# Reordering two chains of block products: phase 2's first two products ahead of phase 1's last two, phase 2 pair by pair, and its operands' preparation in place and queued

## Chip, core and metric

The kernel runs on one core of one Trainium2 chip. Its time is device microseconds (us) of that core, the median of several executions. Time before the change: 851.96 us, median of 3 runs (849.39, 851.96, 854.7). The profile is of one execution of 852.34 us whose span, first to last instruction, is 850.6 us.

## The reference

The reference is a linear attention followed by a two-layer network with a gated activation, over 8 batches of 576 tokens, 8 heads of width 64:

```python
q_s = softmax(q, axis=-1)            # with + 1e-9 in the divisor
k_s = softmax(k, axis=2)             # over the tokens
kv  = einsum('bhsd,bhse->bhde', k_s, v)
x   = einsum('bhsd,bhde->bhse', q_s, kv)   # -> 4608 tokens x 512
h   = x @ w_in                        # 512 x 2048
g   = h * clip(h + 3, 0, 6) / 6
out = g @ w_out                       # 2048 x 512
```

The result is float32. The kernel multiplies each float32 operand as a high and a low part, so one product of blocks takes three matmul passes (high x high, and the two mixed ones).

## The kernel before, in words

**Two halves.** The first 1536 tokens (three blocks of 512) are multiplied plainly by the functions `gemm1` and `gemm2`, while weights are decoded and sums of weight blocks are made and written to DRAM. The other 3072 tokens are three *superblocks* s = 0, 1, 2 of 1024 tokens, and the loop `for s in range(NS)` at the end of the kernel (L796 to L814) runs `phase1(s, between1)` and then `phase2(s, between2)` for each.

**Products.** In a superblock each of the two matrix products is done over 2x2 blocks with seven block products instead of eight, on sums and differences of blocks. The 2048 middle columns are eight pairs p = 0..7, so each phase has 8 x 7 = 56 *slots* (p, n), n being the kind of product. A slot is six TensorE matmuls of 128x512: two column halves c times three passes m. The order of phase 1's slots is SLOTS1 (L393 to L395); it ends with (6,6), (7,4), (7,5), (7,6). Product (7,5) adds onto the PSUM bank in which (7,4) left its sum, after VectorE has read that sum at L554. The order of phase 2's slots is SLOTS2 (L396, L397): all eight pairs of kind 1, then of kind 2, 3, 0, 4, 6, 5. TensorE keeps the program's order from the second block on (`keep_in_program_order`, L79 to L93).

**Phase 1** multiplies weights (fetched from DRAM two slots at a time, six such groups ahead, `fetch` L457) by *factors*: seven tiles `right0` to `right6` made of the superblock's x by `factors(s)` (L482). Its results go from PSUM into the tiles g of pair p (`ga`, `gb`, four quarters a, b, c, d): copies by ScalarE (L545, L550, L552), additions by VectorE (L547, L554, L558), the gated activation `relu6` (L513 ScalarE, L514 VectorE) and a difference (L561).

**Phase 2** multiplies weights by *parts of g*. `make()` (L571) takes the next slot of SLOTS2, splits one quarter of g into high (ScalarE cast, L120) and low (VectorE subtraction, L121) into a ring of four buffers `gf`, and for kinds 1, 2 and 0 does one more VectorE operation on g in place (L582, L584, L586). `make()` is called three times ahead and then once per slot. Sums gather in PSUM: kinds 1, 3, 4 and 5 one after the other in the same two banks `xb`, kind 2 in two banks `yb`, kinds 0 and 6 in two banks `zb`. After pair 7 of a kind, the banks are read: ScalarE scales them into SBUF (L631, L637), VectorE adds two such tiles (L640) or scales and adds (`blend`, L602), and a DMA on SyncE's queue sends results out (`send`, L597). The SBUF tiles for that come from a pool named `v` with three buffers.

**Factors of the next superblock.** `factors(s+1)` is a generator of seven steps. In the order before: split X11; split X21; take a tile from the pool `v`, subtract into it (L497) and split it (T3); subtract twice in place (L500, L501) and split (T2); split (T1); split X22; subtract (L508) and split (T4). A split of such a tile is a ScalarE cast and a VectorE subtraction of 128x1024. A step is called after phase 2's slots 18, 21, 33, 36, 39, 42 and 45 (L808). The steps of the next superblock's attention (`sb_attention(s+1)`, 12 tiles of 128x1024 in all over the three) are called after the odd slots of phase 1 and the first odd ones of phase 2.

**Who sets the order.** TensorE's order is the program's. The order of VectorE's, ScalarE's and GpSimdE's instructions is laid down beforehand by a planner (`schedule_with_timeline_sim=True`, L872) that puts an instruction early where, by its own estimates, the engine is free and the operands are there; what stands in `tc.high_priority()` (the readings of PSUM) goes first. In the trace, three splits of factors (`right<-x`, L121) that the program calls after phase 2's slots 18, 21 and 42 run at 435.34, 437.64 and 447.89 us, the first two ahead of phase 2's first product.

Of the kernel before, what the change touches and what calls it, by code (L numbers as in the profile page):

```python
# [10 lines left out]
F32 = mybir.dt.float32  # L11
# [7 lines left out]
P = 128  # L19
# [13 lines left out]
def attention_moe(  # L33
# [39 lines left out]
    def bank(name):  # L73
        return ps.tile([P, TB], F32, name=name, tag="p")
# [42 lines left out]
    whole = dr.tile([P, NFC, 2 * DM], F32, name="whole")  # L117

    def split(hi, lo, src):
        nc.scalar.copy(hi, src)  # L120
        nc.vector.tensor_sub(lo, src, hi.bitcast(F32))  # L121

    def load_w(f):
        raws[f] = place(f, U32, f"raw_{f}")
# [268 lines left out]
    AT = {1: 0, 0: 1, 3: 3, 2: 4, 4: 6, 5: 9, 6: 12}  # L393
    SLOTS1 = sorted((7 * p + AT[n], p, n) for p in range(NPAIR) for n in range(7))
    SLOTS1 = [(p, n) for _, p, n in SLOTS1]  # L395
    ORDER2 = (1, 2, 3, 0, 4, 6, 5)  # L396
    SLOTS2 = [(p, n) for n in ORDER2 for p in range(NPAIR)]  # L397
    SLOT = [{pn: i for i, pn in enumerate(slots)} for slots in (SLOTS1, SLOTS2)]
    NSLOT = len(SLOTS1)

# [16 lines left out]
    def sum_weights(pair, side):  # L417
# [30 lines left out]
    ring = []  # L448

    come = {}  # L450
    wanted = iter(
        [(s, side, g) for s in range(NS) for side in range(2) for g in range(NSLOT // GROUP)]
    )

    turn = iter(range(10**6))
# [26 lines left out]
    def factors(s):  # L482

        x = x_of(s)
        x11, x12, x21, x22 = (x[:, 2 * a : 2 * a + 2, b * TH : (b + 1) * TH] for a in (0, 1) for b in (0, 1))

        def parts(n, src):
            t = place(n, F32R, f"right{n}").rearrange("p (e i n) -> p e i n", e=2, i=2)
            split(t[:, 0], t[:, 1], src)
            x_parts[s, n] = t  # L490

        parts(X11, x11)
        yield
        parts(X21, x21)
        yield
        t = moe.tile([P, 2 * DM], F32, name="v", bufs=3).rearrange("p (i n) -> p i n", i=2)
        nc.vector.tensor_sub(t, x22, x12)  # L497
        parts(T3, t)
        yield
        nc.vector.tensor_sub(x12, x12, x11)  # L500
        nc.vector.tensor_sub(x11, x22, x12)  # L501
        parts(T2, x11)
        yield
        parts(T1, x12)
        yield
        parts(X22, x22)
        yield
        nc.vector.tensor_sub(x21, x21, x11)  # L508
        parts(T4, x21)
        yield  # L510
# [2 lines left out]
        nc.scalar.activation(r, h, AF.Relu, bias=three, scale=1.0)  # L513
        nc.vector.scalar_tensor_tensor(g, r, 6.0, h, op0=ALU.min, op1=ALU.mult)  # L514

    def phase1(s, between):
        xb, yb, zb = {}, {}, {}
        for i, (p, n) in enumerate(SLOTS1):
            if n == 1:
                xb[p] = bank("x1")[:, 0:TH]  # L520
            if n == 2:
                yb[p] = bank("y1")[:, 0:TH]
            if n == 0:
                zb[p] = bank("z1")[:, 0:TH]
            to = zb[p] if n == 0 else yb[p] if n in (2, 6) else xb[p]
            w_hi, w_lo = (left(s, 0, i)[:, e] for e in (0, 1))
            f_hi, f_lo = (x_parts[s, ORDER[n][1]][:, e] for e in (0, 1))
            for c in range(2):
                cs = slice(c * P, (c + 1) * P)
                for m, (w_, f_) in enumerate(((w_hi, f_hi), (w_hi, f_lo), (w_lo, f_hi))):  # L530
                    mm(to, w_[:, cs], f_[:, c], n in (0, 1, 2) and not c and not m, c == 1 and m == 2, True)
            used(s, 0, i)
            if (s, p) not in g_pairs:
                t = place(7 + p, F32, f"g{p}")
                g_pairs[s, p] = t.rearrange("p (e n) -> p e n", e=2)
            ga, gb = (g_pairs[s, p][:, e] for e in (0, 1))
            h11, h12, h21, h22 = ga[:, 0:TH], ga[:, TH:], gb[:, 0:TH], gb[:, TH:]
            x, y, z = xb.get(p), yb.get(p), zb.get(p)

            def temp():  # L540
                return moe.tile([P, TB], F32, name="g", bufs=2)

            with tc.high_priority():
                if n == 1:
                    nc.scalar.copy(h11, x)  # L545
                if n == 0:
                    nc.vector.tensor_add(h11, h11, z)  # L547
                    relu6(h11, temp(), h11)
                if n == 3:
                    nc.scalar.copy(h21, x)  # L550
                if n == 2:
                    nc.scalar.copy(h22, y)  # L552
                if n == 4:
                    nc.vector.tensor_add(h22, h22, x)  # L554
                if n == 5:
                    relu6(h12, temp(), x)
                if n == 6:
                    nc.vector.tensor_add(h21, h21, y)  # L558
                    r = moe.tile([P, 2 * DM], F32, name="v", bufs=3)
                    relu6(gb, r, gb)  # L560
                    nc.vector.tensor_sub(h12, h22, h12)  # L561
            between(i)

    def phase2(s, between):
        if "g" not in held:
            held["g"] = xp.tile([P, 4, 2, TH], F32R, name="gf", tag="xa")
        ring = held["g"]
# [3 lines left out]
        def make():  # L571
            i, (p, n) = next(made, (None, (None, None)))
            if i is None:
                return
            ga, gb = (g_pairs[s, p][:, e] for e in (0, 1))
            a, b, c, d = ga[:, 0:TH], ga[:, TH:], gb[:, 0:TH], gb[:, TH:]
            src = {1: a, 2: b, 3: a, 0: c, 4: b, 6: c, 5: d}[n]
            t = ring[:, i % 4]
            split(t[:, 0], t[:, 1], src)
            ready[i] = t  # L580
            if n == 1:
                nc.vector.tensor_add(a, a, b)  # L582
            if n == 2:
                nc.vector.tensor_sub(b, d, a)  # L584
            if n == 0:
                nc.vector.tensor_sub(c, c, a)  # L586

        for _ in range(3):
            make()
        xb = [bank("x2")[:, 0:TH] for _ in range(2)]  # L590
        yb = zb = None
        sixth = 1.0 / 6.0
# [12 lines left out]
        for i, (p, n) in enumerate(SLOTS2):  # L605
            if p == 0 and n == 2:
                yb = [bank("y2")[:, 0:TH] for _ in range(2)]
            if p == 0 and n in (0, 6):
                zb = [bank("z2")[:, 0:TH] for _ in range(2)]
            to = zb if n in (0, 6) else yb if n == 2 else xb  # L610
            make()
            f_hi, f_lo = (ready[i][:, e] for e in (0, 1))
            w_hi, w_lo = (left(s, 1, i)[:, e] for e in (0, 1))
            for m, (w_, f_) in enumerate(((w_hi, f_hi), (w_lo, f_hi), (w_hi, f_lo))):
                for c in range(2):
                    mm(
                        to[c],
                        w_[:, c * P : (c + 1) * P],
                        f_,
                        p == 0 and m == 0 and n in (0, 1, 2, 6),  # L620
                        p == NPAIR - 1 and m == 2,
                        True,
                    )
            del ready[i]
            used(s, 1, i)
            if p == NPAIR - 1:
                with tc.high_priority():
                    if n in (1, 3, 5):
                        t = kept_out[n] = outs("o")
                        for c in range(2):  # L630
                            nc.scalar.mul(t[:, c], xb[c], sixth)  # L631
                        if n == 5:
                            send(t, 0, 1)
                    if n == 2:
                        t = kept_out[4] = outs("o")
                        for c in range(2):
                            nc.scalar.mul(t[:, c], yb[c], sixth)  # L637
                    if n == 3:
                        for c in range(2):
                            nc.vector.tensor_add(kept_out[3][:, c], kept_out[3][:, c], kept_out[4][:, c])  # L640
                    if n == 0:
                        for c in range(2):
                            blend(kept_out[1], zb, c)
                        send(kept_out[1], 0, 0)
                    if n == 4:
                        for c in range(2):
                            blend(kept_out[4], xb, c)
                        send(kept_out[4], 1, 1)
                    if n == 6:
                        for c in range(2):  # L650
                            blend(kept_out[3], zb, c)
                        send(kept_out[3], 1, 0)
            between(i)

# [139 lines left out]
    for s in range(NS):  # L796
        more = s + 1 < NS
        step = steps(sb_attention(s + 1), 6) if more else iter(())
        fac = factors(s + 1) if more else iter(())

        def between1(i):
            if i % 2:
                next(step, None)

        def between2(i):
            if i % 2 and i < 16:
                next(step, None)
            if i in (18, 21, 33, 36, 39, 42, 45):  # L808
                next(fac, None)

        phase1(s, between1)
        phase2(s, between2)
        for _ in fac:
            pass  # L814

# [62 lines left out]
```

## Time and profile before

| | |
|---|---|
| time, median of 3 | 851.96 us |
| the profiled execution, span | 852.34 us, 850.6 us |
| TensorE busy | 807.8 us (95%) |
| VectorE busy | 677.9 us (80%) |
| ScalarE busy | 442.6 us (52%) |
| phase 1, s = 0: first product | 347.67 us |
| phase 2: first product, s = 0, 1, 2 | 445.62, 614.22, 769.38 us |
| last matmul's start (phase 2 of s = 2) | about 845.5 us |

How to read it: PE is TensorE's matmuls, PEld its weight loads, DVE VectorE, ACT ScalarE, POOL GpSimdE, SP SyncE with the DMA queue. A line of a group or of the timeline names the source line, the engine, the operation, and written and read tiles by the program's names (x, y and z are the PSUM banks; `right` a factor, `gf` a part of g; `gp` and `left` are the buffers of fetched weights). `x6` is a count of instructions; what stands in brackets is the engine's idle time ahead of that line and what ended it. Matmuls overlap in the records: one is shown with some 390 ns, but the next starts about 0.227 us after it. A row of the chain that ended last gives start, length and what ran.

### The profile page before, as it was taken

How to read it: one execution, taken by the hardware profiler on the slowest of the kernel's cores; microseconds unless marked ns; L12 is line 12 of the kernel's file. 1: busy time of each engine (PE TensorE's matmuls, PEld its weight loads, DVE VectorE, ACT ScalarE, POOL GpSimd, SP SyncE). 2: the span in 40 equal slices, each digit the busy share in tenths (PEclk: the TensorE clock that was granted, in tenths of full speed). 3: DMA queues.
4: the chain of work that ended last, by engine and by line, in shares of the span. 5: the costliest groups of instructions: out<-in, count | busy, mean ns of one | idle time of the engine just before them, and what ended most of it. 6: DMA issues, size and time to landing. Idle time of an engine off the chain costs nothing.

```text
span 850.6 us, 11778 instructions
## 1 busy us (share of the span) xinstructions
PE 807.8 (95%) x4032; PEld 646.5 (76%) x4032; DVE 677.9 (80%) x1095; ACT 442.6 (52%) x717; POOL 66.1 (8%) x179
## 2 busy tenths in 40 slices
PE   4899989999999998999989999999999999999997
PEld 3677767777887786787768868777788788887886
DVE  7998998998878887589889984698688936658763
ACT  7997664443444553444546553545554535445542
POOL 5000011111101110001112000010000000000000
PEclk9999999999999999999999999999999999999999
DMA  9998686578469641788756667664556676665672
GB/s 367 413 401 298 236 272 207 192 263 274 149 201 344 221 165 52 226 279 288 267 177 198 193 215 237 220 227 158 166 189 194 229 241 195 198 195 176 199 234 87
DMA packets 75643, 192.30 MB, mean 226 GB/s; under 512 B 7232, under 2 KB 19520, under 8 KB 73536
## 3 DMA queue, kind: packets, MB, share of 16 engines
q1 hardware_dynamic: 75008, 190.51, 65.7%
q10 hardware_dynamic: 576, 1.05, 0.3%
q8 instruction: 32, 0.52, 0.3%
q14 instruction: 27, 0.22, 0.1%
HBM read 147.49 MB, written 44.04 MB: 225 GB/s over the span
## 4 chain that ended last, share of the span: by engine, by line
PE 63%; DVE 21%; DMA 5%; ACT 4%; issue 4%; POOL 2%; SPq 0%; ACTq 0%; DVEq 0%; POOLq 0%
PE x L87 26%; PE y L87 10%; PE z L87 9%; PE po L87 8%; PE ph L87 8%; DVE gp L121 2%; DVE g L514 2%; DMA qt<-in_qf_dram 2%; PE px L87 2%; POOL swap L303 2%; DVE v L141 1%; DMA kt<-in_kT_dram 1%; DVE v L145 1%; ACT qt L219 1%; PE pkv L87 1%
## 5 line engine op out<-in xcount | busy, mean ns | idle before, releaser
L120 ACT CAST gf<-g 128x512 fp32r<-128x512 f32 x168 | 104.1, 623 | 96.4 <-DVE gf L121 48.5
L87 PE MATMUL po<-w,gp 128*128 128x512 f32 x576 | 146.7, 401 | 5.5 <-ACT gp L120 2.8
L87 PE MATMUL ph<-x,w 128*128 128x512 f32 x576 | 143.8, 397 | 2.9 <-ACT w L120 2.6
L121 DVE TENSOR_TENSOR gf<-g,gf 128x512 fp32r<-128x512 f32 x168 | 112.9, 686 | 31.9 <-ACT gf L120 31.1
L87 PEld LDWEIGHTS po<-w,gp 128*128 128x128 f32 x576 | 106.0, 189 | 33.9 <-ACT gp L120 5.9
L87 PEld LDWEIGHTS ph<-x,w 128*128 128x128 f32 x576 | 108.6, 190 | 28.4 <-ACT w L120 3.3
L87 PE MATMUL x<-right,gp 128*128 128x512 f32 x384 | 96.3, 396 | 3.7 <-DVE g L554 3.7
L87 PE MATMUL x<-gf,gp 128*128 128x512 f32 x384 | 89.0, 389 | 0.0
L87 PEld LDWEIGHTS x<-right,gp 128*128 128x128 f32 x384 | 72.4, 190 | 20.2 <-DVE g L554 4.5
L87 PEld LDWEIGHTS x<-gf,gp 128*128 128x128 f32 x384 | 72.1, 188 | 15.0
L513 ACT ACTIVATE g<-ph,three 128x512 f32<-128x512 f32 x48 | 32.7, 686 | 67.0 <-PE ph L87 66.7
L513 ACT ACTIVATE v<-g,three 128x1024 f32<-128x1024 f32 x24 | 27.6, 1152 | 42.8 <-DVE g L558 42.8
L87 PE MATMUL x<-right,left 128*128 128x512 f32 x192 | 48.0, 393 | 1.7 <-DVE g L554 1.7
L87 PE MATMUL y<-right,gp 128*128 128x512 f32 x192 | 48.4, 397 | 0.0
L87 PE MATMUL z<-gf,gp 128*128 128x512 f32 x192 | 45.7, 392 | 0.9 <-DVE gf L121 0.7
L87 PE MATMUL x<-gf,left 128*128 128x512 f32 x192 | 44.8, 389 | 0.0
L120 ACT CAST gp<-g 128x512 fp32r<-128x512 f32 x48 | 29.7, 620 | 28.0 <-DVE g L514 27.8
L87 PEld LDWEIGHTS z<-gf,gp 128*128 128x128 f32 x192 | 35.7, 188 | 9.9 <-DVE gf L121 2.6
L87 PEld LDWEIGHTS x<-right,left 128*128 128x128 f32 x192 | 35.6, 188 | 10.0 <-DVE g L554 2.5
L87 PEld LDWEIGHTS y<-right,gp 128*128 128x128 f32 x192 | 35.9, 190 | 8.2 <-issue 0.5
L87 PEld LDWEIGHTS x<-gf,left 128*128 128x128 f32 x192 | 36.0, 188 | 7.5
L513 ACT ACTIVATE g<-g,three 128x512 f32<-128x512 f32 x24 | 17.4, 724 | 39.2 <-DVE g L547 39.2
(136 smaller groups left out, 1297.5 us busy)
## 6 DMA issues: line engine op xcount, KB each, us to landing
gp<-wf SPq DMA_DIRECT2D x112, 512.0 KB, 3.5
left<-wf SPq DMA_DIRECT2D x56, 512.0 KB, 3.5
raw<-in_w_dram SPq DMA_DIRECT2D x16, 1024.0 KB, 13.7
wf<-gp SPq DMA_DIRECT2D x64, 256.0 KB, 3.0
wf<-w SPq DMA_DIRECT2D x48, 256.0 KB, 4.1
vt<-in_v_dram SPq DMA_DIRECT2D x28, 325.0 KB, 5.7
kt<-in_kT_dram SPq DMA_DIRECT2D x28, 288.0 KB, 3.4
ke<-in_k_dram SPq DMA_DIRECT2D x24, 320.0 KB, 5.2
```

What stands on the lines that cost most here:

```text
L87: nc.tensor.matmul(out, lhsT, rhs, start=start, stop=stop, skip_group_check=goes_on)
L120: nc.scalar.copy(hi, src)
L121: nc.vector.tensor_sub(lo, src, hi.bitcast(F32))
L141: nc.vector.scalar_tensor_tensor(vu, high, 0xC0000000, m, op0=ALU.bitwise_and, op1=ALU.bitwise_or)
L145: nc.vector.tensor_tensor(vu, vu, low, op=ALU.add)
L219: nc.scalar.activation(qs[:, i], qs[:, i], AF.Exp, bias=qm[:, i : i + 1], accum_out=qr[:, i : i + 1],)
L303: nc.gpsimd.tensor_copy(swap[r : r + QD], stat[o : o + QD])
L513: nc.scalar.activation(r, h, AF.Relu, bias=three, scale=1.0)
L514: nc.vector.scalar_tensor_tensor(g, r, 6.0, h, op0=ALU.min, op1=ALU.mult)
```

## The change

Five edits, all in the superblocks:

1. **Order of the phases.** The functions `phase1` and `phase2` become generators that stop after each slot, and one list PHASES runs both: phase 1's slots 0 to 53, then phase 2's slots 0 and 1, then phase 1's slots 54 and 55 ((7,5) and (7,6)), then phase 2's from 2 on. The order in which weights are fetched follows that list. The first three `make()` are called ahead of phase 1's slot 50.
2. **Order of phase 2.** All pairs of kind 1; then pair by pair kinds 2 and 3 in turn; then pair by pair kinds 0 and 4; then kind 6; then kind 5.
3. **Factors without a temporary.** T1 = x12 - x11 and T2 = x22 - T1 are made in place, in the tile of x11, and T3 = x22 - x12 in that of x12; the order of steps is X11, X21, T1, T2, T3, X22, T4. There are as many operations as before (four subtractions, seven splits).
4. **Where factor steps are called.** After phase 2's slots 9, 13, 17, 23, 29, 35 and 41.
5. **Queued.** Each such step is traced inside `tc.issue_after` of the cast and the subtraction that the latest `make()` returned (`front`): none of the step's instructions may be planned ahead of them on ScalarE or VectorE. The factors of superblock 0, made during the plain blocks, have edit 3 but not this one.

```diff
     def split(hi, lo, src):
-        nc.scalar.copy(hi, src)
-        nc.vector.tensor_sub(lo, src, hi.bitcast(F32))
+        return nc.scalar.copy(hi, src), nc.vector.tensor_sub(lo, src, hi.bitcast(F32))
+
+    front = []
+
+    def behind(units, count=1):
+
+        with ExitStack() as order:
+            for ins in front:
+                order.enter_context(tc.issue_after(ins.ins))
+            for _ in range(count):
+                next(units, None)
...
-    ORDER2 = (1, 2, 3, 0, 4, 6, 5)
-    SLOTS2 = [(p, n) for n in ORDER2 for p in range(NPAIR)]
+    ORDER2 = ((1,), (2, 3), (0, 4), (6,), (5,))
+    SLOTS2 = [(p, n) for some in ORDER2 for p in range(NPAIR) for n in some]
...
+    PHASES = [(0, i) for i in range(NSLOT)] + [(1, i) for i in range(NSLOT)]
+    PHASES[NSLOT - 2 : NSLOT + 2] = PHASES[NSLOT : NSLOT + 2] + PHASES[NSLOT - 2 : NSLOT]
     wanted = iter(
-        [(s, side, g) for s in range(NS) for side in range(2) for g in range(NSLOT // GROUP)]
+        [(s, side, i // GROUP) for s in range(NS) for side, i in PHASES if i % GROUP == 0]
     )
...
         parts(X21, x21)
         yield
-        t = moe.tile([P, 2 * DM], F32, name="v", bufs=3).rearrange("p (i n) -> p i n", i=2)
-        nc.vector.tensor_sub(t, x22, x12)
-        parts(T3, t)
-        yield
-        nc.vector.tensor_sub(x12, x12, x11)
-        nc.vector.tensor_sub(x11, x22, x12)
+        nc.vector.tensor_sub(x11, x12, x11)
+        parts(T1, x11)
+        yield
+        nc.vector.tensor_sub(x11, x22, x11)
         parts(T2, x11)
         yield
-        parts(T1, x12)
+        nc.vector.tensor_sub(x12, x22, x12)
+        parts(T3, x12)
         yield
...
-            split(t[:, 0], t[:, 1], src)
+            front[:] = split(t[:, 0], t[:, 1], src)
...
         for _ in range(3):
             make()
+        yield
         xb = [bank("x2")[:, 0:TH] for _ in range(2)]
...
-        def between1(i):
-            if i % 2:
+        phases = phase1(s), phase2(s)
+        for side, i in PHASES:
+            if (side, i) == (0, NSLOT - 6):
+                next(phases[1])
+            next(phases[side])
+            if i % 2 and (not side or i < 16):
                 next(step, None)
-
-        def between2(i):
-            if i % 2 and i < 16:
-                next(step, None)
-            if i in (18, 21, 33, 36, 39, 42, 45):
-                next(fac, None)
-
-        phase1(s, between1)
-        phase2(s, between2)
+            if side and i in (9, 13, 17, 23, 29, 35, 41):
+                behind(fac)
         for _ in fac:
             pass
```

More of the change, by code (lines that the diff above doesn't have):

```diff
@@ L514, in relu6, with phase1 @@
         nc.vector.scalar_tensor_tensor(g, r, 6.0, h, op0=ALU.min, op1=ALU.mult)
-    def phase1(s, between):
+    def phase1(s):
         xb, yb, zb = {}, {}, {}
@@ L561, in phase1, with phase2 @@
                     nc.vector.tensor_sub(h12, h22, h12)
-            between(i)
-    def phase2(s, between):
+            yield
+    def phase2(s):
         if "g" not in held:
@@ L652, in phase2 @@
                         send(kept_out[3], 1, 0)
-            between(i)
+            yield
     def gemm1(j, f):
```

## The prediction

> **What bounds the kernel now.** I read the page first, then the chain that ended last, then the timelines of TensorE and VectorE in the superblocks.
>
> ```profile
> PE 807.8 (95%) x4032; PEld 646.5 (76%) x4032; DVE 677.9 (80%) x1095; ACT 442.6 (52%) x717; POOL 66.1 (8%) x179
> PE 63%; DVE 21%; DMA 5%; ACT 4%; issue 4%; POOL 2%; SPq 0%; ACTq 0%; DVEq 0%; POOLq 0%
> ```
>
> TensorE is the bound, and the change takes no matmul away. What can be won is TensorE's waiting in the superblocks, which comes in two kinds.
>
> **Inside phase 2.** The chain shows each phase 2 from its first product to the start of kind 5, its last eight slots:
>
> ```profile
> 445.79 10.88 PE x L87 x48
> ...
> 490.43 5.27 DMA out_dram<-v
> ...
> 514.13 12.24 PE x L87 x54
> ...
> 614.38 10.88 PE x L87 x48
> 625.26 10.88 PE y L87 x48
> ...
> 681.33 12.24 PE x L87 x54
> ...
> 769.54 10.88 PE x L87 x48
> ...
> 834.82 10.67 PE x L87 x47
> ```
>
> Eight slots take 10.88 us, so one takes 1.36 and six runs 65.28. For s = 2, which makes no factors, the distance is 834.82 - 769.54 = 65.28: no loss. For s = 0 it is 68.34, a loss of 3.06; for s = 1 66.95, a loss of 1.67. VectorE's timeline and its waits between 445 and 700 us say what was late:
>
> ```profile
> 495.80 1.23 DVE L497 TENSOR_TENSOR v<-x 128x1024 f32<-128x1024 f32 x1 [2.84 <-DMA out_dram<-v]
> ...
> 503.29 1.29 DVE L121 TENSOR_TENSOR gf<-g,gf 128x512 fp32r<-128x512 f32 x2
> ```
> ```profile
> DVE gf L121 <- ACT gf L120: 14.0, 23, 0.8
> ...
> DVE v L497 <- DMA out_dram<-v: 4.3, 2, 2.8
> ```
>
> L497 wants a buffer of the pool `v` that an output DMA still reads; VectorE stands 4.3 us in the two superblocks together, then pays for four factors one after the other, and the parts of g stand behind them.
>
> **At the end of phase 1.** TensorE's timeline from (7,4) to phase 2's first product, for s = 0, 1, 2:
>
> ```profile
> 436.90 1.55 PE L87 MATMUL x<-right,gp 128*128 128x512 f32 x6
> 441.27 2.93 PE L87 MATMUL x<-right,gp 128*128 128x512 f32 x6 [2.82 <-DVE g L554]
> 443.99 1.79 PE L87 MATMUL y<-right,gp 128*128 128x512 f32 x6
> 445.62 2.65 PE L87 MATMUL x<-gf,gp 128*128 128x512 f32 x11
> ```
> ```profile
> 608.95 1.52 PE L87 MATMUL x<-right,gp 128*128 128x512 f32 x6
> 611.32 1.67 PE L87 MATMUL x<-right,gp 128*128 128x512 f32 x6 [0.85 <-DVE g L554]
> ...
> 614.22 4.02 PE L87 MATMUL x<-gf,left 128*128 128x512 f32 x17
> ```
> ```profile
> 764.13 1.52 PE L87 MATMUL x<-right,left 128*128 128x512 f32 x6
> ...
> 769.38 2.88 PE L87 MATMUL x<-gf,gp 128*128 128x512 f32 x12
> ```
>
> Three slots are due there, 4.08 us. They took 8.72, 5.27 and 5.25: losses of 4.64, 1.19 and 1.17, 7.00 in all. Each time (7,5) waits for L554 to read the bank that (7,4) has just filled. For s = 0 that reading is late, because VectorE runs behind, with factors planned in between:
>
> ```profile
> 435.34 1.22 DVE L121 TENSOR_TENSOR right<-x,right 128x1024 fp32r<-128x1024 f32 x1
> 436.48 1.23 DVE L321 STREAM_TRANSPOSE m<-qt 128x1024 f32<-128x1024 f32 x1
> 437.64 1.18 DVE L121 TENSOR_TENSOR right<-x,right 128x1024 fp32r<-128x1024 f32 x1
> 438.74 0.68 DVE L514 SCALAR_TENSOR_TENSOR g<-g,g 128x512 f32<-128x512 f32 x1
> 439.34 0.68 DVE L514 SCALAR_TENSOR_TENSOR g<-g,x 128x512 f32<-128x512 f32 x1
> ...
> 440.54 0.68 DVE L554 TENSOR_TENSOR g<-g,x 128x512 f32<-128x512 f32 x1
> ...
> 447.89 1.22 DVE L121 TENSOR_TENSOR right<-x,right 128x1024 fp32r<-128x1024 f32 x1
> ```
>
> From start to start VectorE spends 0.60 us on 512 columns and 1.14 on 1024; those are the prices below. The most that the change can win in these places is 7.00 + 3.06 + 1.67 = **11.7 us**.
>
> **The change part by part.**
>
> *Phase 2's first two products ahead of (7,5).* They put 2.72 us between (7,4) and (7,5). L554 needs 0.85 us of waiting where VectorE is free, so for s = 1 and 2 the wait disappears: 1.19 + 1.17 won. They need the parts of pairs 0 and 1, whose quarter of g has been final since early in phase 1; with four free ring buffers the planner can make them there, off the path. If that cover were gone, each would cost a cast and a subtraction of 0.6 us. For s = 0 the wait of 2.82 is just covered, and the first two factors (2.28 us of VectorE ahead of L554) leave that place too. So all 4.64 go from the boundary, part of which is the clock:
>
> ```profile
> 441.00:445.00 4.00, 2.72 (x5) 0.57 0.19 77
> ...
> 445.62:470.00 24.38, 23.54 (x39) 1.00 0.59 189
> ```
>
> These rows give VectorE's busy time, then the granted TensorE clock: 0.57 right behind the wait, 1.00 after it. (7,5) took 2.72 us and (7,6) 1.63 where 1.36 each is due, and 4.64 - 2.82 = 1.8 us is that slowness with the restart. [...]
>
> *What is late next in s = 0.* The second row above is the price: behind the boundary VectorE was busy 23.54 of 24.38 us and just kept up with TensorE, which waited for nothing there. TensorE now arrives 4.64 us earlier. VectorE is relieved by three factor splits (3.4 us); by slot 18 the alternation with kind 3 has put off three of kind 2's extra operations (1.8); X11 and X21 come back behind the parts of slots 12 and 16 (-2.28). That is 2.9 us of relief against 4.64. The bounds are no loss, if the parts have slack enough, and the whole 4.64, if they have none and the relief lies elsewhere. I take **2.0**, near the difference of 1.7, with some added for T1, which follows soon after.
>
> *Kinds in turn.* Kinds 1, 2 and 0 cost VectorE 1.20 us a slot, the others 0.60, against TensorE's 1.36. In turn they cost 0.90. With factors at the new places, the parts of slots 8 to 39 need 32 x 0.60 + 16 x 0.60 = 28.8; X11, X21, X22 3.4; T1, T2, T3 at 2.28 each 6.8; L640 and the first blend four operations, 2.4. That makes 41.4 of the 43.5 us that TensorE takes, in a stretch where parts are made up to three slots ahead. It fits narrowly. Bounds: nothing, or a factor's cast waited out each time (below). For s = 0 it is in the 2.0; for s = 1 I take **0.4**. The late slots with 0.60 each hold T4 easily.
>
> *Handing over bank x.* Kind 3 adds onto the banks of kind 1, and kind 4 onto those of kind 3. Before, eight slots of another kind lay between; now one does. What reads the banks is ScalarE:
>
> ```profile
> 624.84 0.62 ACT L120 CAST gf<-g 128x512 fp32r<-128x512 f32 x1 [0.73 <-PE x L87]
> 625.37 1.08 ACT L631 ACTIVATE v<-x 128x512 f32<-128x512 f32 x2
> 626.34 0.62 ACT L120 CAST gf<-g 128x512 fp32r<-128x512 f32 x1
> ```
>
> Kind 1 ends at 625.26 (the start of y in the chain), both banks are read by 626.45, and kind 3 would start at 626.62, its second bank at 626.85. So the handover fits with 0.2 to 0.4 us to spare. If one more cast stands ahead, it is 0.53 later and 0.1 to 0.3 is lost; nothing is won. At six handovers I take 0.1 each, **0.6**.
>
> *Factors without the temporary.* Four subtractions and seven splits as before, on tiles of the same size: no cost. The 4.3 us of waiting for an output DMA go, as no factor takes a buffer of `v`. With the steps spread out, the losses of 3.06 and 1.67 go.
>
> *Queued behind `front`.* No operation is added; the engines run in a laid-down order and the edge only keeps the planner from pulling factors ahead of parts. The order of the DMAs is re-sorted, with the same number. Superblock 0's factors, made in the plain blocks, have the same work in another order. TensorE waits there too:
>
> ```profile
> 326.77 1.20 PE L87 MATMUL po<-w,gp 128*128 128x512 f32 x4 [2.23 <-DVE gp L121]
> ```
>
> That place can gain or lose 2.2 us; I take nothing.
>
> *Sum.* 11.7 - 2.0 - 0.4 - 0.6 = 8.7 us off the profiled execution's 852.34 (span 850.6 and 1.7 around it): 843.6. That execution is 0.4 above the median of the runs shown, so against the median I forecast **843.3**.
>
> **The rivals.**
>
> *All of it is won.* VectorE catches up because the planner moves more than I counted: 851.96 - 11.7 = 840.3. For it: s = 2 shows a phase 2 without loss. Against: 23.54 of 24.38 us busy.
>
> *The wait of s = 0 moves.* VectorE sets the pace from 426 to 470 us, and TensorE, no longer held at the boundary, waits for parts instead: 4.64 lost in place of 2.0, 846.0. For it: the same row. Against: three factors leave.
>
> *Banks handed over late.* Each handover finds a cast ahead of its readings, and that cast's own start is held up in turn: 0.53 each beyond what I took, six times, 3.2 us, 846.5. [...]
>
> *VectorE waits out each factor's cast (slower than before).* The subtraction that ends a split needs ScalarE's cast of the same tile:
>
> ```profile
> L120 ACT CAST right<-x 128x1024 fp32r<-128x1024 f32 x18 | 18.6, 1051 | 6.4 <-DVE x L501 3.8 <-DVE x L508 2.1 <-DVE x L500 0.5
> 496.00:510.00 14.00, 14.00 (x18) 1.00 0.59 194
> ```
>
> If the planner puts nothing between them, VectorE idles 1.05 us in each of seven steps, 7.4 a superblock; the narrow stretch has 2.1 spare, so 5.3 are TensorE's, in two superblocks 10.6, and the time is 843.3 + 10.6 = 853.9. From 6.5 us of idling in each it is slower than before. For it: 14.0 us of waits for the casts of parts. Against: the second row, where VectorE was busy 14.00 of 14.00 us amid factors, with parts between.
>
> *It doesn't do what it says.* The edge sets only an earliest place; if the planner then delays factors until they pile up late, or pulls attention into the freed places, the losses stay: about 851.
>
> **How the numbers follow.** A measurement of this kernel can tell about 1% from no change, 8.5 us, so below 843.4 is faster and above 860.5 slower. Chances: forecast 0.50 (its own range 841.5 to 845.5), all won 0.12, wait moves 0.14, banks late 0.08, casts waited out 0.10, not what it says 0.06. The forecast stands at the border, so I give half of it, a little more, to faster: 0.28 + 0.12 + 0.03 from the others' lower ends = 0.43. Slower by over 1% needs the slower rival and another loss of 6.6 us: 0.06. The rest, 0.51, lies within 1%. The range goes from 840.0, all won, to 851.5, where the losses stay; above it lies most of the slower rival.
>
> **What would show it.** Right: phase 1's (7,5) without a wait for L554 in all three superblocks and no clock below 1.00 there; no L497 waiting for an output DMA; kind 6 of s = 0 and 1 without waits for parts; small waits for parts around slots 12 to 24 of s = 0, some 2 us. Wrong: waits of kind 3's or 4's first product for L631 of over 0.3 us; VectorE idle ahead of `right` by a cast's length; phase 2 of s = 1 over 77 us; any of the boundary's waits still there.

## The result, and the profile after

The changed kernel takes 841.47 us (median of 6 runs, 838.82 to 845.34) beside 852.15 us before (6 runs): a ratio of 0.9876, 95% interval 0.9844 to 0.9908. It is 10.7 us faster, 1.2%; 843.3 was forecast. The profiled execution took 839.71 us, with a span of 837.9.

The line numbers moved: L554 of before is L565 now (L564 or L566 in some experiments), both halves of a split are L120, the reduction over the queries (L311) is L320, the reading of bank x (L631) L643.

TensorE's timeline at the end of phase 1, for s = 0, 1 and 2, each from (7,4) on, and the start of kind 5 in the first two:

```profile
433.75 1.52 PE L87 MATMUL x<-right,gp 128*128 128x512 f32 x6
435.11 2.88 PE L87 MATMUL x<-gf,gp 128*128 128x512 f32 x12
438.41 1.65 PE L87 MATMUL x<-right,gp 128*128 128x512 f32 x6 [0.42 <-DVE g L565]
439.90 1.52 PE L87 MATMUL y<-right,gp 128*128 128x512 f32 x6
441.26 2.88 PE L87 MATMUL x<-gf,gp 128*128 128x512 f32 x12
...
505.10 5.60 PE L87 MATMUL x<-gf,gp 128*128 128x512 f32 x24
```
```profile
600.10 1.52 PE L87 MATMUL x<-right,gp 128*128 128x512 f32 x6
601.46 2.88 PE L87 MATMUL x<-gf,gp 128*128 128x512 f32 x12
604.18 1.52 PE L87 MATMUL x<-right,left 128*128 128x512 f32 x6
605.54 1.52 PE L87 MATMUL y<-right,left 128*128 128x512 f32 x6
...
669.56 1.75 PE L87 MATMUL x<-gf,left 128*128 128x512 f32 x7
```
```profile
752.52 1.52 PE L87 MATMUL x<-right,left 128*128 128x512 f32 x6
753.88 2.88 PE L87 MATMUL x<-gf,left 128*128 128x512 f32 x12
756.60 1.52 PE L87 MATMUL x<-right,gp 128*128 128x512 f32 x6
```

For s = 1 and 2 every slot of these lines follows the one before by 1.36 us; the two `gf` products stand between (7,4) and (7,5) and nothing waits. For s = 0 a wait of 0.42 is left of 2.82. The waits of TensorE from 420 us on are two (second fence), where there were eight (first fence); a line gives the total, the number and the longest in us:

```profile
PE x L87 <- DVE g L554: 5.4, 4, 2.8
PE z L87 <- DVE gf L121: 2.4, 4, 1.2
```
```profile
PE x L87 <- DVE g L565: 0.4, 1, 0.4
PE x L87 <- DVE gf L120: 0.4, 1, 0.4
```

**One measure for all runs.** From the first matmul of (7,4) to the first of kind 5 there are 51 slots, 69.36 us without loss. For s = 0 the kernel before took 436.90 to 513.96, this one 433.75 to 505.10:

```profile
513.96 2.20 PE L87 MATMUL x<-gf,gp 128*128 128x512 f32 x9
```

| us | s = 0 | s = 1 | s = 2 | sum |
|---|---|---|---|---|
| loss before | 7.70 | 2.86 | 1.17 | 11.73 |
| loss after | 1.99 | 0.10 | 0.15 | 2.24 |
| won | 5.71 | 2.76 | 1.02 | 9.49 |

Of the 1.99 us that s = 0 still lost, 0.71 lie at (7,5), with the wait of 0.42 there, and 1.09 at two slots of kind 3, phase 2's slots 13 and 17, whose parts came late. The first of the two:

```profile
457.73 0.73 PE L87 MATMUL x<-gf,gp 128*128 128x512 f32 x2 [0.40 <-DVE gf L120]
```

The two profiled executions differ by 12.63 us. 9.49 lie here; 1.29 lie ahead of the first superblock product (347.67 before, 346.38 now), and 1.87 in phase 1 of s = 0 (from its first product to (7,4): 89.23 us before, 87.36 now). The stretch of s = 1 (84.11 and 84.12), that of s = 2 (72.08 in both) and the end (15.9 us from s = 2's kind 5 to the last instruction, in both) did not move.

### The profile page after: what moved, and what is told of

It is laid out like the page before. It is cut to its first block, busy times and chain, and to the rows that moved or that the text cites. A ratio compares the mean times of both kernels' runs of the same rounds, so it can differ in the third digit from the quotient of the medians.

```text
span 837.9 us, 11778 instructions
## 1 busy us (share of the span) xinstructions
PE 805.7 (96%) x4032; PEld 648.1 (77%) x4032; DVE 677.7 (81%) x1095; ACT 442.4 (53%) x717; POOL 68.0 (8%) x179
## 4 chain that ended last, share of the span: by engine, by line
PE 67%; DVE 18%; DMA 5%; ACT 4%; issue 3%; POOL 2%; SPq 0%; ACTq 0%; DVEq 0%; POOLq 0%
PE x L87 30%; PE z L87 12%; PE y L87 11%; PE po L87 6%; PE ph L87 5%; PE px L87 2%; DVE gp L120 2%; POOL swap L312 2%; DVE g L525 2%; PE pkv L87 1%; DVE v L150 1%; DVE v L154 1%; DMA v<-whole 1%; DMA qt<-in_qf_dram 1%; ACT qt L228 1%
## 5 line engine op out<-in xcount | busy, mean ns | idle before, releaser
L120 ACT CAST gf<-g 128x512 fp32r<-128x512 f32 x168 | 104.4, 623 | 95.2 <-DVE gf L120 34.9
L120 DVE TENSOR_TENSOR gf<-g,gf 128x512 fp32r<-128x512 f32 x168 | 112.9, 685 | 26.2 <-ACT gf L120 25.4
L87 PE MATMUL x<-gf,gp 128*128 128x512 f32 x384 | 94.0, 390 | 0.4 <-DVE gf L120 0.4
L87 PE MATMUL x<-gf,left 128*128 128x512 f32 x192 | 47.3, 390 | 0.1
L120 ACT CAST gp<-g 128x512 fp32r<-128x512 f32 x48 | 29.7, 619 | 25.5 <-DVE g L525 25.3
```

Source lines behind the costliest of these rows:

```text
L87: nc.tensor.matmul(out, lhsT, rhs, start=start, stop=stop, skip_group_check=goes_on)
L120: return nc.scalar.copy(hi, src), nc.vector.tensor_sub(lo, src, hi.bitcast(F32))
```

## The experiments

Medians are compared with the kernel before on the same chip (851.06 to 851.55 us beside e1 to e12); the losses are by the measure above, in one profiled execution each. How far a loss of s = 0 would repeat in another execution of the same program, no run shows; s = 2's loss in the five programs with the phases in turn (before, e1, e6, e9, e10) is 1.15 to 1.29 us. In all of them the end and s = 2's phase 1 are as before; phase 1 of s = 0 began between 345.5 and 351.2 us, with no relation to the edits that I could find.

| run | median us | ratio to before, interval | s = 0 | s = 1 | s = 2 |
|---|---|---|---|---|---|
| before | 852.15 | | 7.70 | 2.86 | 1.17 |
| the change | 841.47 | 0.9876, 0.9844 to 0.9908 | 1.99 | 0.10 | 0.15 |
| without the swap (e1) | 845.08 | 0.9916, 0.9887 to 0.9944 | 5.98 | 1.24 | 1.29 |
| kinds one by one (e2) | 844.67 | 0.9906, 0.9869 to 0.9943 | 3.81 | 0.00 | 0.00 |
| not queued (e3) | 851.61 | 1.0009, 0.9988 to 1.0030 | 8.89 | 4.23 | 0.11 |
| with the temporary (e4) | 843.13 | 0.9904, 0.9872 to 0.9937 | 3.28 | 0.11 | 0.11 |
| before + swap (e5) | 847.44 | 0.9953, 0.9934 to 0.9973 | 4.86 | 1.90 | 0.00 |
| before + in place (e6) | 856.48 | 1.0063, 1.0046 to 1.0080 | 11.26 | 3.28 | 1.19 |
| extra VectorE work (e7) | 854.81 | 1.0043, 1.0027 to 1.0059 | 11.21 | 3.35 | 0.13 |
| later places (e8) | 841.92 | 0.9879, 0.9847 to 0.9910 | 1.04 | 0.11 | 0.13 |
| before + queue (e9) | 851.50 | 0.9996, 0.9972 to 1.0020 | 6.94 | 2.02 | 1.15 |
| e1, attention queued (e10) | 844.88 | 0.9913, 0.9883 to 0.9943 | 1.31 | 1.30 | 1.25 |
| e8, attention queued (e11) | 842.16 | 0.9879, 0.9846 to 0.9911 | 0.13 | 0.13 | 0.14 |
| e8, attention behind slot 40 (e12) | 841.52 | 0.9877, 0.9844 to 0.9910 | 1.88 | 0.13 | 0.13 |

The theory, as the prediction has it: TensorE loses time where VectorE reads a bank or makes a part of g too late; the swap covers the reading, and spreading and queueing the factors keeps the parts in time, with VectorE's throughput just sufficient. The rivals are that one of these pieces does nothing.

**Undoing one part each.**

*Without the swap (e1).*

```diff
-    PHASES[NSLOT - 2 : NSLOT + 2] = PHASES[NSLOT : NSLOT + 2] + PHASES[NSLOT - 2 : NSLOT]
```

> The change without the swap: phase 1 runs to its end, then phase 2. My theory: (7,5) waits for L565 (L554 before) again whatever else is done, so the stretch from (7,4) to kind 5 loses 1.0 to 1.2 us more in s = 1 and 2, and 1.2 to 3 us more in s = 0; in all 3.4 to 5.4 us over the changed kernel, about 845.5 us. Rival: the boundary lost time only because factors were pulled ahead of it; with them queued the wait is 0.3 us or less in each, and the time stays within 1 us of the changed kernel's.

s = 1 and 2 lost 1.14 more each, as the theory says, and the rival falls. But s = 0 lost 4.0 more, over the expected 1.2 to 3. TensorE's and VectorE's timelines there:

```profile
438.27 2.33 PE L87 MATMUL x<-right,gp 128*128 128x512 f32 x6 [3.94 <-DVE g L564]
```
```profile
433.59 0.68 DVE L568 TENSOR_TENSOR g<-g,y 128x512 f32<-128x512 f32 x1
436.40 1.22 DVE L320 TENSOR_REDUCE qm<-qt 128x32 f32<-128x1024 f32 x1 [2.13 <-DMA qt<-in_qf_dram]
437.54 0.68 DVE L564 TENSOR_TENSOR g<-g,x 128x512 f32<-128x512 f32 x1
```

No factor stands there any more. What stands ahead of the reading of (7,4)'s bank is the reduction over the queries of the superblock after next, planned early into the free place, and it waits 2.13 us for its DMA. The changed kernel has the same wait (1.91 us at L320) and the two products cover all of it but 0.42.

*Kinds one by one (e2).*

```diff
-    ORDER2 = ((1,), (2, 3), (0, 4), (6,), (5,))
+    ORDER2 = ((1,), (2,), (3,), (0,), (4,), (6,), (5,))
```

> The change with phase 2's order of before (kinds 1, 2, 3, 0, 4, 6, 5, each over all pairs), factors at the new places and queued. My theory: VectorE has 1.20 us a slot in slots 0 to 15 and 24 to 31 and the factors at 9, 13, 23 and 29 come on top, so TensorE waits for parts: s = 0 loses 3 to 5 us in place of 2.0, s = 1 1 to 2 us in place of 0.1; 2 to 5 us in all. Rival: parts made three slots ahead absorb it, the order of kinds does nothing, and the losses stay at 2.0 and 0.1 us within 0.5.

Half right: s = 0 lost 1.8 us more, 1.28 of it waiting for one part of kind 2. s = 1 lost nothing at all; there the alternation isn't needed. The handover to kind 4, which costs the changed kernel 0.08 us each, is gone too.

```profile
462.42 1.88 PE L87 MATMUL y<-gf,gp 128*128 128x512 f32 x7 [1.28 <-DVE gf L120]
```

*Not queued (e3).*

```diff
-                behind(fac)
+                next(fac, None)
```

> The change with factor steps called at the same places but not queued behind the parts. My theory: the planner pulls X11, X21 and X22 ahead of phase 2 again, and VectorE reads (7,4)'s bank later: s = 0 loses 1 to 3 us more, s = 1 up to 1. Rival: the swap's 2.7 us of cover and the in-place factors are enough, and the time stays within 0.5 us.

Far more than I expected: 6.9 and 4.1 us, the whole gain of the change. VectorE's timeline in s = 0 shows why (the program calls these steps after slots 9 to 41, and slot 2 ran at about 443 us):

```profile
441.45 1.23 DVE L514 TENSOR_TENSOR x<-x 128x1024 f32<-128x1024 f32 x1
442.60 1.22 DVE L120 TENSOR_TENSOR right<-x,right 128x1024 fp32r<-128x1024 f32 x1
...
447.41 1.21 DVE L120 TENSOR_TENSOR right<-x,right 128x1024 fp32r<-128x1024 f32 x1
448.55 1.21 DVE L511 TENSOR_TENSOR x<-x 128x1024 f32<-128x1024 f32 x1
449.68 1.21 DVE L120 TENSOR_TENSOR right<-x,right 128x1024 fp32r<-128x1024 f32 x1
450.82 0.68 DVE L593 TENSOR_TENSOR g<-g 128x512 f32<-128x512 f32 x1
451.42 0.68 DVE L120 TENSOR_TENSOR gf<-g,gf 128x512 fp32r<-128x512 f32 x1
```
```profile
452.15 1.20 PE L87 MATMUL x<-gf,left 128*128 128x512 f32 x4 [3.08 <-DVE gf L120]
```

Five factor operations of 1024 columns run within 9.5 us, three of them in a row ahead of L593 and the split of one part of g (451.42 us), and TensorE waits 3.08 us for that part. All eleven factor operations of s = 0 begin by 464.3 us here. In the kernel before the third step needed a buffer of the pool `v`, which an output had to leave first, and it and the seven operations behind it ran from 495.80 us on.

*With the temporary (e4)*: the changed kernel with the lines of `factors` of before (in the diff of the change, the lines with a minus).

> The change with the factors as before (T3 through a temporary of the pool v, then T2, T1), at the new places and queued. My theory: the temporary waits for an output DMA, or holds a buffer that a reading of bank x wants, and s = 0 and s = 1 lose 1.5 to 3 us each. Rival: at slot 17 only one of the three buffers is taken, nothing waits, the losses stay within 0.5 us; the wait for the DMA was a matter of the late place, not of the temporary.

The rival is right on the superblocks' wait: the subtraction into the temporary (L509, at 467.72 us) follows the part ahead of it without a gap, and VectorE's list of waits has no output DMA.

```profile
466.52 1.28 DVE L120 TENSOR_TENSOR gf<-g,gf 128x512 fp32r<-128x512 f32 x2
467.72 1.22 DVE L509 TENSOR_TENSOR v<-x 128x1024 f32<-128x1024 f32 x1
```

The 1.3 us more in s = 0 lie partly at (7,5), ahead of every factor (1.2 us there for 0.6). Only in the plain blocks does the old order show: the wait of 2.23 us behind factors of superblock 0 is back, which the change had cut to 0.19. All four programs with the old order of the factors have it (before, e4, e5, e9: 2.2 us), and none of the ten with the new one (0.2).

```profile
325.91 2.07 PE L87 MATMUL po<-w,gp 128*128 128x512 f32 x4 [2.24 <-DVE gp L120]
```

**Doing one part alone.**

*Before + swap (e5)*: the changed kernel with old order, old places, old factors, no queue.

> The kernel before with the swap alone (factors with the temporary, at the old places, not queued, old order of kinds). My theory: s = 1 and 2 win their 1.0 to 1.2 us at the boundary; s = 0 wins part of its 4.6 there (factors are still planned ahead of L554's reading), and the losses behind late parts in kind 6 stay (1.5 to 3 us in s = 0 and 1). From (7,4) to kind 5: 4 to 7 us in s = 0, 1.5 to 2 in s = 1, about 0.1 in s = 2, some 846 to 849 us. Rival: TensorE, arriving earlier, only waits for parts instead, and s = 0 and 1 lose what they lost before (7.7 and 2.9).

In size as expected in all three; s = 2 lost nothing, s = 0 4.86, and 847.44 us lies in the range given. The rival falls in s = 1 and 2. In s = 0 it holds in part: of the 4.64 us at the boundary 4.25 were won, but 2.6 were lost again in kinds 1 to 3, behind late parts (waits of 1.21 and 0.43 us), where the kernel before lost nothing. Kind 6 lost 1.75 in place of 3.01.

```profile
455.00 2.11 PE L87 MATMUL x<-gf,left 128*128 128x512 f32 x8 [1.21 <-DVE gf L120]
```

*Before + in place (e6)*: old order, places and boundary, no queue, the new `factors`.

> The kernel before with the factors made in place alone (no swap, old places, not queued, old order of kinds). Theory after the run without the queue: the temporary held four of the seven factors back until an output DMA had freed its buffer; without it the planner pulls all seven to the end of phase 1, ahead of the parts, and s = 0 and s = 1 lose more than before: 8 to 12 us and 4 to 6 us, about 855. Theory of the prediction: the waits for the DMA go (4.3 us) and with them the losses in kind 6, s = 0 loses about 5, s = 1 about 1.3, some 848 us.

s = 0 lost 11.26, the kernel 5.3 us: slower than before, as the theory after e3 says, and not the 848 us that follow from the prediction's reading. s = 1 lost 3.28, less than the 4 to 6. All eleven factor operations of s = 0 begin by 463.1 us, and three of them stand ahead of the reading of (7,4)'s bank; the last of the three, the reading, and TensorE's wait for it:

```profile
440.54 1.22 DVE L507 TENSOR_TENSOR x<-x 128x1024 f32<-128x1024 f32 x1
...
442.27 0.68 DVE L564 TENSOR_TENSOR g<-g,x 128x512 f32<-128x512 f32 x1
```
```profile
443.01 2.93 PE L87 MATMUL x<-right,gp 128*128 128x512 f32 x6 [3.98 <-DVE g L564]
```

*Before + queue (e9)*: old factors, order and places, phases in turn, with `behind`.

> The kernel before with the queue alone: factor steps with the temporary, at the old places (after slots 18, 21, 33, 36, 39, 42, 45), behind the parts; no swap, old order of kinds. Theory: the queue keeps X11, X21 and X22 from the end of phase 1, but seven steps now run between slots 21 and 48, of which 24 to 31 are heavy, and the temporary still waits for a DMA: at the boundary s = 0 loses what the run with the phases in turn lost (4 to 5 us, behind the query's reduction), s = 1 and 2 1.2 each, and inside phase 2 s = 0 and 1 lose 1 to 4 us each; in all 8 to 13 us, as before or a little less, 848 to 853 us. Rival: the queue alone carries the win, and the losses fall under 7 us.

10.1 us of loss, 851.5 us: no gain that can be told. The rival falls. Here VectorE again waited for an output DMA, 3.3 us in two waits, at the old, late places.

**Is VectorE's time the narrow thing? (e7)**

```diff
+            if n in (3, 4):
+                nc.vector.tensor_add(moe.tile([P, TB], F32, name="g", bufs=2), a, d)
```

> The changed kernel with one VectorE addition of 512 columns more, into a scratch tile that nothing reads, for each slot of kinds 3 and 4: 16 in each superblock, 9.6 us of VectorE in slots 8 to 39. My theory, VectorE's throughput is the narrow thing there (41.4 of 43.5 us): s = 1 loses 3 to 6 us in place of 0.1, s = 0 7 to 10 in place of 2.0, and s = 2, which makes no factors and has 13 us to spare, at most 0.5. Rival, only the order of VectorE's instructions matters and it has time enough: all three stay within 1 us of the changed kernel.

s = 1 lost 3.25 more, s = 2 nothing; s = 0 lost 9.2 more, a little over the range. The stretches from the start of slot 8 to that of slot 40, in s = 0, 1 and 2, give TensorE's, its weight loads' and VectorE's busy time, first with the extra work, then in the changed kernel:

```profile
452.90:505.85 52.95, 47.20 (x193) 34.95 (x192) 52.11 (x80) 28.22 (x45) 4.81 (x4) 1.00 0.54 157
626.74:673.57 46.83, 45.26 (x194) 35.47 (x192) 46.83 (x71) 28.02 (x45) 0.00 (x0) 1.00 0.63 180
782.41:826.06 43.65, 43.65 (x193) 35.96 (x192) 40.11 (x66) 22.56 (x39) 0.00 (x0) 1.00 0.66 194
```
```profile
449.42:494.22 44.80, 44.26 (x194) 35.80 (x192) 43.96 (x67) 27.83 (x45) 1.67 (x4) 1.00 0.59 187
615.06:658.68 43.62, 43.62 (x194) 35.95 (x192) 41.96 (x61) 27.72 (x45) 0.00 (x0) 1.00 0.61 193
767.48:811.14 43.66, 43.66 (x193) 35.95 (x192) 33.76 (x52) 22.55 (x39) 0.00 (x0) 1.00 0.61 193
```

With the extra work VectorE fills s = 1's stretch entirely (46.83 of 46.83), and the stretch is 3.2 us longer; in s = 2 VectorE comes to 40.11 of 43.65 and TensorE loses nothing. In the changed kernel s = 1 stands at 41.96 of 43.62, where the prediction worked out 41.4 of 43.5, and s = 0 at 43.96 of 44.80: nearly full, and just in time.

**What is left, and whether it can be had.**

*Later places (e8)*: the factor steps after slots 17, 21, 25, 29, 33, 37, 41.

> The changed kernel with the factor steps after slots 17, 21, 25, 29, 33, 37 and 41. My theory: the two waits for parts near slots 11 and 15 of s = 0 come from X11 and X21 standing between parts while VectorE is behind; put off, they go, and s = 0 loses 0.7 to 1.2 us in place of 2.0, the others as in the changed kernel, unless four subtracting steps in a row now cost s = 1 0.5 to 1 us. Rival: VectorE is behind from the attention's work planned there, and the waits stay at 2.0.

s = 0 lost 1.04 in place of 1.99 and no part came late any more; what stayed is 0.50 at (7,5). In the time, 841.92 us, it doesn't show.

*e1 with the attention queued (e10), e8 with it queued (e11).*

```diff
-                next(step, None)
+                behind(step)
```

> The run with the phases in turn (the change without the swap), with the attention steps queued as the factors are: those of the superblock after next can't be planned ahead of phase 2's last part. Theory: what held (7,4)'s bank for 3.9 us in s = 0 was the reduction of the next queries (L320), planned ahead of it and waiting for its DMA; without it s = 0 loses 1.2 us at the boundary as s = 1 and 2 do, and nothing in phase 2, in all about 3.6 us. Rival, the prediction's: s = 0 is late there because VectorE has too much work before it, and still loses over 3 us.

> The changed kernel with the later places of the factor steps (17, 21, 25, 29, 33, 37, 41) and the attention steps queued too. Theory: with the attention of s = 2 out of the end of s = 0, all three superblocks lose 0.3 us or less from (7,4) to kind 5, so 1.7 us less than the changed kernel, if s = 1's phase 1, which takes that work, stays at 84.1 us to (7,4). Rival: the work moved into s = 1's phase 1 costs TensorE there what it saves in s = 0, and the time is the changed kernel's or worse.

e10 settles the boundary of s = 0: with the reduction out of the way it loses 1.31, as the others do, of which 0.85 is the wait that s = 1 and 2 of the kernel before show for that reading too. The time hardly follows, 844.88 us beside e1's 845.08: the work put off falls into s = 1's phase 1, which to (7,4) takes 87.04 us in place of e1's 84.61.

```profile
434.82 1.52 PE L87 MATMUL x<-right,gp 128*128 128x512 f32 x6
437.19 1.66 PE L87 MATMUL x<-right,gp 128*128 128x512 f32 x6 [0.85 <-DVE g L564]
```

In e11 all three superblocks lose 0.13 or 0.14, and the rival is right all the same: s = 1's phase 1 to (7,4) takes 86.55 us in place of 84.12, since the moved work now holds ScalarE's readings there (the attention's exponential, L323, runs from 517.78 us, right ahead of the first of the two).

```profile
519.37 1.66 PE L87 MATMUL x<-right,gp 128*128 128x512 f32 x6 [0.73 <-ACT g L556]
520.87 1.53 PE L87 MATMUL y<-right,gp 128*128 128x512 f32 x6
523.14 1.21 PE L87 MATMUL x<-right,gp 128*128 128x512 f32 x4 [0.75 <-ACT g L561]
```

*Attention behind slot 40's part (e12)*: e8 with this; `light` is empty until then.

```diff
-                next(step, None)
+                behind(step, light)
+            if side and i == 37:
+                light[:] = front
```

> The changed kernel with the later places of the factor steps, and the attention steps of the superblock after next queued behind the part of slot 40 of phase 2, from where on VectorE has 0.60 us a slot to do against TensorE's 1.36. Theory: the planner fills those light slots with that attention; s = 0 loses 0.3 us or less from (7,4) to kind 5 and s = 1's phase 1 to (7,4) stays within 0.5 us of 84.1, so about 2 us less than the changed kernel from the first superblock product on. Rival: the work lands in s = 1's phase 1 all the same (86 us or more), and nothing is won.

Neither: s = 0 lost 1.88, now in kind 6 (0.78 waiting for a part at 494.58 us) with another 0.7 in kind 5, and s = 1's phase 1 took 85.16. Of the versions tried none beats the changed kernel beyond the intervals; they move the same 2 us about.

## Why the prediction was right, and where its reasons were not

**The size.** It gave 8.7 us: 11.7 less 2.0, 0.4 and 0.6. Measured in the same places: 11.73 less 1.99, 0.10 and 0.15 in the three superblocks, 9.49. The handovers are in these figures and were costed too high: three slots, the first of kind 4 in each superblock, took 1.44 us in place of 1.36 (0.08 each); the first of kind 3 lost nothing. The 2.0 for s = 0 fits partly by luck. Only 1.09 of the 1.99 are the late parts that it stood for; 0.71 lie at (7,5), which the working counted as won. e7 shows that VectorE's time, the reason given for the late parts, is real.

**The swap** did what the working said in s = 1 and 2, by e1 and e5; alone it won 5.0 us of loss (e5, 6.76 in place of 11.73). **Kinds in turn** fit, and are worth 1.8 us, all of it in s = 0 (e2).

**Where a step failed: "Factors without the temporary".** The prediction had the losses in kind 6 go because no factor takes a buffer of `v`, and costed the queue at nothing, as a guard. e4 shows that at the new places the temporary waits for nothing; e6 shows that taking it away *costs* 4.0 us of loss (15.73 in place of 11.73) while nothing else holds the factors. The temporary was a brake that came off too late; the queue is a brake in the right place. The step was right that the edge adds no work, and wrong in what the edge is worth: with the other four edits and no queue, 851.61 us, nothing is won. Nor does the queue alone win anything (e9). What the change won beyond the swap belongs to queue and places together, as far as the runs show: the change with only the old places put back was not run, so the places' own share stays open. In place, the factors are only no longer held late; by e4 that is worth 1.3 us at most.

**The boundary of s = 0.** The prediction put its lateness down to factors planned in between. They stood there; but with them gone (e1) the wait was 3.94 us, longer than the 2.82 of before, since the planner put the reduction of later queries into the freed place. e10 shows that one as the cause in e1. That the change wins 3.9 of these 4.6 us all the same is the swap's cover, not the factors' leaving: e5 won 4.25 there with two splits of factors still at 438.5 and 440.8 us.

**The rivals.** All won: e11 shows that the 11.7 can be had there (0.40 left), at the price of 2.4 us elsewhere. The wait that moves: it stayed at 1.99, not 4.64. Casts waited out: not seen; two splits of factors waited for their casts, 0.25 us in s = 0 and 0.19 in s = 1.

**Not forecast.** 3.2 us between the profiled executions lie ahead of (7,4) of s = 0. The wait of 2.23 us in the plain blocks shrank to 0.19, and e4 ties that to the order of the factors; a new wait of 0.94 us at 343 us gave some of it back. So the working stands behind 9.5 of the 12.6 us between the two profiled executions; the rest came unforecast, and so far the fit is luck. What else moves the start of phase 1 is open: it spreads over 5.7 us between programs whose plain blocks are nearly the same, and I did not find what sets it.

## What to carry to other kernels

Where a planner lays down the engines' order by its own estimates, work without a deadline is pulled into any place that looks free, and on the chip it stands ahead of what the bound engine waits for (3.94 us in e1, 3.08 in e3); say where it must not go, not only where it is called. A buffer that is scarce by accident may be such a fence: before taking it away, ask what it holds back. And measure a change of order by the bound engine's loss between two fixed points of its own program: here that resolved 0.1 us where single executions of one kernel spread over 6.

## What the runs showed of the hardware that was not expected

A wait of TensorE's is followed by half clock in one run and not in another. From start to start across the wait, 3.47 us in e9 was followed by matmuls 0.43 us apart and a granted clock of 0.50; 3.46 us in e3 by matmuls 0.23 us apart and 1.00. The first row is e9's, the second e3's; the granted clock stands third from the right:

```profile
440.90:444.00 3.10, 3.09 (x7) 2.51 (x8) 2.75 (x4) 0.06 (x1) 1.37 (x2) 0.50 0.01 4
```
```profile
452.10:455.50 3.40, 3.35 (x14) 2.53 (x15) 3.40 (x5) 2.28 (x5) 0.00 (x0) 1.00 0.11 17
```

Nor does it take a wait that long. The wait in the plain blocks, 2.23 us in the kernel before and 2.24 in e4, left the clock full there and halved it here:

```profile
326.70:329.00 2.30, 2.23 (x10) 1.84 (x11) 2.30 (x4) 0.62 (x1) 0.00 (x0) 1.00 0.00 0
```
```profile
325.90:328.00 2.10, 2.09 (x5) 1.71 (x6) 2.10 (x3) 0.63 (x1) 0.00 (x0) 0.50 0.00 0
```

The records of the granted clock show a beat. In the traces of the two kernels each spell of half clock ahead of the last matmul lasts 3.41 us, and in the kernel before the clock falls at 28.09, 113.42 and 441.11 us: 85.33 and 327.69 us apart, 25 and 96 times 3.413. How much waiting goes with a fall, and why the clock fell behind one wait and not behind another as long, no run isolates. So the slow matmuls behind such a wait are a cost that may or may not come. In the kernel before they came at the boundary of s = 0 (2.82 us of waiting, a granted clock of 0.50 from 441.11 to 444.52 us); the change's longest wait there is 0.42 us, and the clock stayed at 1.00.
